# Phase two of a three-stage kernel: the sums of weight blocks on DVE instead of GpSimd

## The chip, the cores and the metric

One core of a Trainium2 chip runs the whole program. The metric is the device time of one execution in microseconds (us). Three executions of the kernel before took 1212.9, 1214.16 and 1216.59 us; the median is 1214.16 us.

The engines are called as the profile calls them: PE is TensorE (matmul), PEld its weight loads, DVE is VectorE, ACT is ScalarE, POOL is GpSimd, and SP issues the DMAs.

## The reference

A linear attention with decay is followed by two feed-forward layers. The last one is the second phase of the kernel, and the change lies there:

```python
def _moe2_ref(x, w_gate, w_val, w_out):      # x: 3072 x 512
    gate = 1.0 / (1.0 + np.exp(-(x @ w_gate)))   # 512 x 1536
    val = x @ w_val                              # 512 x 1536
    return (gate * val @ w_out).astype(np.float32)
```

Everything is float32 to the outside. The kernel splits each operand of a large product into a high and a low part and makes three matmuls of them (high by high, high by low, low by high).

## The kernel before

Phase one, to about 655 us of the trace, makes the attention and the first feed-forward layer, and writes its result to DRAM (`x2d`); it also converts the weights of the second layer to float32 and stores them (`w2d`). Phase two reads both back.

In phase two the products with `w_gate` and `w_val` are made by a Strassen-like scheme: seven block products instead of eight, on blocks of 256 columns of weights and on 512 tokens. For this it needs sums of blocks of the weights (S1 to S4) and sums of blocks of the activations (T1 to T4). The unit of work is a **chain**: one gate or value product for two feature blocks and 1024 tokens. There are 36 chains: 3 groups of 1024 tokens, 3 rounds in each, 4 chains in a round (gate, value, gate, value). A chain takes PE seven products of six matmuls, about 9.7 us. After the fourth chain of a round come the products with `w_out` (L651 to L653) for eight token tiles.

What a chain `n` does, in the order in which it is written out by hand (`manual_schedule`; each engine runs its instructions in that order):

- `load_chain(n)` (L493) lets SP issue two DMAs of the weights into one tile `raw8` of eight blocks. Two such tiles exist, one for even and one for odd chains.
- `sums(n)` (L503) makes the sums in place: S3 = A21 - A11 (L506, 256 columns), S1 and S2 in one instruction (L507, 512 columns), S4 = A12 - S2 (L510, 256 columns). Each needs the one before it.
- `split_chain(n, late)` (L512) splits the blocks: ACT rounds to the high part `oh` (L518), and the low part `ol` is the difference (L521). The early half (S1, S2, A11, A12; 1024 columns) has its difference on DVE, the late half (S3, A22, S4; 768 columns) on GpSimd.
- `begin(n)` makes the first product into a PSUM bank `pa`; `middle(n)` makes four more: into `pb`, into `pa` again (S2 by T2), into `pd`, into `pa` again (S3 by T3). Between the last two that use `pa`, ACT copies the bank out to a tile `u` (L588), so the S3 product has to wait for that copy. `finish(n)` makes the last two.
- The four results of a chain are `pb`, `c` (made of `pd` and a tile `u` by the DVE add of L538), `pa` and `pd`. For a gate chain ACT takes the sigmoid of each (L546). For a value chain each is multiplied by its gate on DVE (L555), rounded to `g2h` on ACT (L557), and the rest `g2l` is made on DVE (L559). `g2h` and `g2l` are the stationary operands of L651 to L653.
- The eight output tiles of a round rotate through three PSUM banks `po`; each is evicted by DVE or ACT (L655 to L668), so the fourth tile's products wait for the eviction of the first.
- `split_out2` (L637) splits a block of `w_out`: ACT makes `woh` (L640), GpSimd the low part `wol` (L641).

In iteration `n` of the loop at L798, `sums(n + 2)` is called behind `middle(n)` (L809), that is, right behind the add that makes `c` of chain `n`. For the fourth chain of a group's last round it is called between two evictions instead (L838). `sums(0)` is called in phase one (L780) and `sums(1)` at the border of the phases (L796). So 34 of the 36 calls lie in the loop: 9 in first chains, 9 in second, 8 in third, 6 in fourth chains, and 2 between evictions.

Of the kernel before, what the change touches and what calls it, by code (L numbers as in the profile page):

```python
# [13 lines left out]
ALU = mybir.AluOpType  # L14
# [10 lines left out]
def retention_moe_moe2(  # L25
# [12 lines left out]
    nc = tc.nc  # L38
# [374 lines left out]
    A21, S3, A22, S4, S1, S2, A11, A12 = range(8)  # L413
# [89 lines left out]
    def sums(n):  # L503

        t = wraw8[n]
        nc.gpsimd.tensor_tensor(out=t[:, S3], in0=t[:, A21], in1=t[:, A11], op=ALU.subtract)  # L506
        nc.gpsimd.tensor_tensor(  # L507
            out=t[:, S1:S2 + 1], in0=t[:, A21:S3 + 1], in1=t[:, A22:A22 + 1].to_broadcast([P, 2, 256]), op=ALU.add
        )
        nc.gpsimd.tensor_tensor(out=t[:, S4], in0=t[:, A12], in1=t[:, S2], op=ALU.subtract)  # L510

    def split_chain(n, late):  # L512

# [156 lines left out]
    with tc.manual_schedule():  # L670
# [56 lines left out]
        for i, (b, f) in enumerate(units):  # L727
# [50 lines left out]
            if b == len(blocks1) - 1:  # L778
                if f == 9:
                    sums(0)  # L780
                elif f in (11, 13):
                    split_chain(0, f == 13)()
# [11 lines left out]
        load_out(0)  # L794
        evict1(*units[-1])
        sums(1)  # L796
        xs = iter(())
        for n, (g, r, p, m) in enumerate(chains):  # L798
# [9 lines left out]
            if n + 2 < len(chains) and not (last and r == NR - 1):  # L808
                sums(n + 2)  # L809
# [117 lines left out]
```

## Time and profile before

| | us |
|---|---|
| median of three executions | 1214.16 |
| the profiled execution | 1213.36 |
| its span, first to last instruction | 1211.6 |
| PE busy | 1190.9 (98%) |
| DVE busy | 794.1 (66%) |
| ACT busy | 541.5 (45%) |
| POOL busy | 531.4 (44%) |

The span is 1.76 us shorter than the execution; that rest lies before the first and behind the last instruction. PE is busy nearly throughout, so an instruction on another engine matters only where PE comes to wait for it. Matmuls are pipelined: one is shown 0.39 us long, while the next one starts 0.23 us after it. PE's granted clock is full in all of phase two.

In a row of the timeline stand the start, the duration, the engine, the line, the operation, the tiles as output<-inputs, the shapes, and in brackets the idle time before it with what ended it. A row that ends in x2 is two instructions that followed each other.

### The profile page before, as it was taken

To read this page: it belongs to the slowest core of one execution; us is meant where nothing else is said; L and a number is where in the kernel's file an instruction comes from. 1 tells how busy PE (TensorE), PEld (TensorE's weight loads), DVE (VectorE), ACT (ScalarE), POOL (GpSimd) and SP (SyncE) were. 2 spreads that over 40 slices of the span, in tenths; PEclk is the share of its full clock that TensorE was granted. 3 is DMA by queue.
4 is the path that set the end of the run, shared out by engine and by line. 5 is a ranking of instruction groups with operands and counts; after the bars stand their busy time and mean duration, and the time that the engine had idled before them with its cause. 6 is when DMAs were issued, how large, how long until landed. Compare 5 with 4: busy or idle time off the path is not lost.

```text
span 1211.6 us, 16035 instructions
## 1 busy us (share of the span) xinstructions
PE 1190.9 (98%) x5916; PEld 953.2 (79%) x5916; DVE 794.1 (66%) x1049; ACT 541.5 (45%) x948; POOL 531.4 (44%) x398
## 2 busy tenths in 40 slices
PE   7999999999999999999999999999999999999998
PEld 6656878877788888788788888887888887888887
DVE  5989999686688677766663626367636458535454
ACT  5333444444444445444554526163626163626151
POOL 4556875222332332322454616166625256534340
PEclk8999999999999999999999999999999999999999
DMA  8554344534334334412102202043202142211111
GB/s 318 187 180 141 87 157 164 193 114 137 124 98 163 123 113 141 124 49 86 63 1 87 79 27 79 27 139 105 73 32 75 31 130 89 86 44 59 47 35 70
DMA packets 62431, 123.48 MB, mean 102 GB/s; under 512 B 6800, under 2 KB 16016, under 8 KB 62352
## 3 DMA queue, kind: packets, MB, share of 16 engines
q1 hardware_dynamic: 62352, 122.46, 31.0%
q8 instruction: 46, 0.75, 0.3%
q14 instruction: 33, 0.27, 0.1%
HBM read 98.31 MB, written 24.12 MB: 101 GB/s over the span
## 4 chain that ended last, share of the span: by engine, by line
PE 79%; DVE 10%; POOL 4%; issue 4%; DMA 2%; ACT 1%; SPq 0%; DVEq 0%; POOLq 0%; ACTq 0%
PE pa L529 14%; PE pd L529 7%; PE acc L377 6%; PE h L273 6%; PE h L272 6%; PE h L271 6%; PE acc L378 6%; PE acc L379 6%; PE po L651 4%; PE po L652 4%; PE po L653 4%; PE pb L529 3%; DVE cva L234 3%; PE h L142 2%; DVE cva L231 2%
## 5 line engine op out<-in xcount | busy, mean ns | idle before, releaser
L264 POOL TENSOR_TENSOR wl<-wraw,wh 128x512 fp32r<-128x512 f32 x112 | 163.5, 1466 | 300.8 <-ACT wh L263 300.4
L271 PE MATMUL h<-xh,wh 128*128 128x512 f32 x384 | 155.0, 404 | 0.7 <-ACT xh L187 0.7
L273 PE MATMUL h<-xh,wl 128*128 128x512 f32 x384 | 152.4, 397 | 2.2 <-POOL wl L264 1.9
L272 PE MATMUL h<-xl,wh 128*128 128x512 f32 x384 | 151.4, 394 | 0.2 <-DVE xl L188 0.2
L377 PE MATMUL acc<-gh,wh 128*128 128x512 f32 x352 | 142.2, 404 | 1.4 <-DVE half L396 1.4
L378 PE MATMUL acc<-gh,wl 128*128 128x512 f32 x352 | 137.9, 392 | 0.0
L379 PE MATMUL acc<-gl,wh 128*128 128x512 f32 x352 | 137.2, 390 | 0.0
L263 ACT CAST wh<-wraw 128x512 fp32r<-128x512 f32 x184 | 109.4, 616 | 35.5 <-PE acc L379 35.0
L521 POOL TENSOR_TENSOR ol<-raw,oh 128x768 fp32r<-128x768 f32 x36 | 68.0, 1889 | 127.1 <-ACT oh L518 127.1
L281 ACT ACTIVATE sg<-h 128x512 f32<-128x512 f32 x88 | 52.6, 598 | 146.6 <-PE h L273 146.4
L282 DVE TENSOR_TENSOR sg<-h,sg 128x512 f32<-128x512 f32 x88 | 60.6, 688 | 86.6 <-ACT sg L281 86.3
L651 PE MATMUL po<-woh,g2h 128*128 128x512 f32 x288 | 113.1, 393 | 2.8 <-DVE ost L538 2.8
L529 PE MATMUL pa<-xol,oh 128*128 128x512 f32 x288 | 114.0, 396 | 0.0
L529 PE MATMUL pa<-xoh,oh 128*128 128x512 f32 x288 | 113.3, 394 | 0.0
L529 PE MATMUL pa<-xoh,ol 128*128 128x512 f32 x288 | 112.8, 392 | 0.0
L652 PE MATMUL po<-wol,g2h 128*128 128x512 f32 x288 | 112.5, 390 | 0.0
L653 PE MATMUL po<-woh,g2l 128*128 128x512 f32 x288 | 112.3, 390 | 0.0
L287 ACT CAST gh<-sg 128x512 fp32r<-128x512 f32 x88 | 54.6, 621 | 98.1 <-DVE sg L282 98.1
L641 POOL TENSOR_TENSOR wol<-wor,woh 128x512 fp32r<-128x512 f32 x36 | 56.9, 1581 | 89.6 <-ACT woh L640 89.6
L273 PEld LDWEIGHTS h<-xh,wl 128*128 128x128 f32 x384 | 72.4, 189 | 21.7 <-POOL wl L264 5.2
L271 PEld LDWEIGHTS h<-xh,wh 128*128 128x128 f32 x384 | 72.7, 189 | 18.9 <-issue 1.0
L272 PEld LDWEIGHTS h<-xl,wh 128*128 128x128 f32 x384 | 72.5, 189 | 18.2 <-issue 1.9
(122 smaller groups left out, 2521.3 us busy)
## 6 DMA issues: line engine op xcount, KB each, us to landing
w<-in_w_dram SPq DMA_DIRECT2D x68, 512.0 KB, 3.7
in_t<-in_qkv_dram SPq DMA_DIRECT2D x96, 256.0 KB, 3.3
raw<-w2d SPq DMA_DIRECT2D x72, 256.0 KB, 3.1
w2d<-cva SPq DMA_DIRECT2D x36, 256.0 KB, 2.2
wor<-w2d SPq DMA_DIRECT2D x36, 256.0 KB, 2.7
out_dram<-ost SPq DMA_DIRECT2D x24, 256.0 KB, 2.0
xt<-x2d SPq DMA_DIRECT2D x18, 256.0 KB, 4.4
x2d<-ost SPq DMA_DIRECT2D x14, 256.0 KB, 2.9
```

Source lines behind the costliest of these rows:

```text
L263: nc.scalar.copy(wh, raw)
L264: lo_engine.tensor_tensor(out=wl, in0=raw, in1=wh, op=ALU.subtract)
L271: nc.tensor.matmul(bank[:, :n], wh[:, k, :], xh[:, k, :n], start=(k == 0), stop=False)
L272: nc.tensor.matmul(bank[:, :n], wh[:, k, :], xl[:, k, :n], start=False, stop=False)
L273: nc.tensor.matmul(bank[:, :n], wl[:, k, :], xh[:, k, :n], start=False, stop=(k == KC - 1))
L377: nc.tensor.matmul(a, wh[:, wc], gh[:, :n], start=st, stop=False)
L378: nc.tensor.matmul(a, wl[:, wc], gh[:, :n], start=False, stop=False)
L379: nc.tensor.matmul(a, wh[:, wc], gl[:, :n], start=False, stop=sp)
L529: nc.tensor.matmul(bank, w[:, kk], x[:, k, :], start=start and k == 0 and w is wh and x is xh, stop=stop and k == 1 and w is wl, skip_grou ...
L651: nc.tensor.matmul(bank, gh, wh, start=f == 0, stop=False)
L652: nc.tensor.matmul(bank, gh, wl, start=False, stop=False)
L653: nc.tensor.matmul(bank, gl, wh, start=False, stop=f == FR - 1)
```

## The change

All three instructions of `sums` are made on DVE (`nc.vector`) instead of GpSimd (`nc.gpsimd`). Operands, order and places of the calls stay.

```diff
     def sums(n):
 
         t = wraw8[n]
-        nc.gpsimd.tensor_tensor(out=t[:, S3], in0=t[:, A21], in1=t[:, A11], op=ALU.subtract)
-        nc.gpsimd.tensor_tensor(
+        nc.vector.tensor_tensor(out=t[:, S3], in0=t[:, A21], in1=t[:, A11], op=ALU.subtract)
+        nc.vector.tensor_tensor(
             out=t[:, S1:S2 + 1], in0=t[:, A21:S3 + 1], in1=t[:, A22:A22 + 1].to_broadcast([P, 2, 256]), op=ALU.add
         )
-        nc.gpsimd.tensor_tensor(out=t[:, S4], in0=t[:, A12], in1=t[:, S2], op=ALU.subtract)
+        nc.vector.tensor_tensor(out=t[:, S4], in0=t[:, A12], in1=t[:, S2], op=ALU.subtract)
```

## Rows read from the trace of the kernel before

**Rows 1.** Busy time by window in phase two; columns as in its first line.
```profile
core 0: us, PE busy (x) PEld busy (x) DVE busy (x) ACT busy (x) POOL busy (x), PEclk, DMA share, GB/s
640.00:800.00 160.00, 160.00 (x697) 130.62 (x696) 78.10 (x97) 70.33 (x116) 71.26 (x57) 1.00 0.20 61
800.00:1206.00 406.00, 403.19 (x1745) 326.68 (x1744) 223.29 (x282) 176.53 (x294) 189.43 (x144) 1.00 0.23 72
```

**Rows 2.** Waits of PE from 640 us on: total us, times, longest.
```profile
PE po L651 <- DVE ost L538: 2.8, 6, 0.9
```

**Rows 3.** Groups by line and shape, GpSimd: busy us, mean ns, idle before.
```profile
L507 POOL TENSOR_TENSOR raw<-raw 128x512 f32<-128x512 f32 x36 | 46.6, 1296 | 2.8
```

**Rows 4.** Three DVE lines: duration in ns, min/median/max, and shape.
```profile
L699 DVE TENSOR_TENSOR dv_sb<-dv_sb,dc_sb x4: 166/168/169, 9.2 to 9.8; 128x8 f32<-128x8 f32 x4
L254 DVE TENSOR_TENSOR cva<-cva,cvb x36: 676/684/690, 191.7 to 562.8; 128x512 f32<-128x512 f32 x36
L521 DVE TENSOR_TENSOR ol<-raw,oh x36: 1214/1215/1226, 629.6 to 1172.0; 128x1024 fp32r<-128x1024 f32 x36
```

**Rows 5.** Timeline of DVE and GpSimd where both want SBUF at once.
```profile
814.92 2.23 DVE L469 TENSOR_TENSOR xol<-xt,xoh 128x512 fp32r<-128x512 f32 x2
816.65 1.64 POOL L641 TENSOR_TENSOR wol<-wor,woh 128x512 fp32r<-128x512 f32 x1 [0.65 <-ACT woh L640]
817.07 1.77 DVE L555 TENSOR_TENSOR c<-c,sg 128x512 f32<-128x512 f32 x1
```

**Rows 6.** Timeline of PE where a bank came late.
```profile
830.41 0.39 PE L653 MATMUL po<-woh,g2l 128*128 128x512 f32 x1
831.18 0.50 PE L651 MATMUL po<-woh,g2h 128*128 128x512 f32 x1 [0.38 <-DVE ost L538]
831.98 0.40 PE L651 MATMUL po<-woh,g2h 128*128 128x512 f32 x1
```

**Rows 7.** Timeline of DVE in a fourth chain (group 1, round 1).
```profile
692.85 0.69 DVE L538 TENSOR_TENSOR c<-pd,u 128x512 f32<-128x512 f32 x1 [1.10 <-ACT u L598]
693.57 1.81 DVE L555 TENSOR_TENSOR c<-c,sg 128x512 f32<-128x512 f32 x1
696.34 0.70 DVE L555 TENSOR_TENSOR pa<-pa,sg 128x512 f32<-128x512 f32 x1 [0.96 <-PE pa L529]
697.70 0.69 DVE L559 TENSOR_TENSOR g2l<-pa,g2h 128x512 fp32r<-128x512 f32 x1 [0.65 <-ACT g2h L557]
700.99 0.68 DVE L661 COPY part<-po 128x512 f32<-128x512 f32 x1
```

**Rows 8.** GpSimd and ACT in that chain.
```profile
692.72 0.75 POOL L506 TENSOR_TENSOR raw<-raw 128x256 f32<-128x256 f32 x1 [0.81 <-DMA raw<-w2d]
693.45 0.62 ACT L640 CAST woh<-wor 128x512 fp32r<-128x512 f32 x1
```

**Rows 9.** PE's weight loads in that chain.
```profile
699.86 0.19 PEld L653 LDWEIGHTS po<-woh,g2l 128*128 128x128 f32 x1
702.80 0.19 PEld L651 LDWEIGHTS po<-woh,g2h 128*128 128x128 f32 x1
```

**Rows 10.** Timeline of DVE in a second chain (group 1, round 3).
```profile
788.59 0.70 DVE L538 TENSOR_TENSOR pd<-pd,u 128x512 f32<-128x512 f32 x1 [2.80 <-PE pd L529]
...
794.86 0.69 DVE L538 TENSOR_TENSOR c<-pd,u 128x512 f32<-128x512 f32 x1 [1.10 <-ACT u L598]
...
797.59 1.91 DVE L559 TENSOR_TENSOR g2l<-c,g2h 128x512 fp32r<-128x512 f32 x1
799.42 0.69 DVE L538 TENSOR_TENSOR pd<-pd,u 128x512 f32<-128x512 f32 x1
```

**Rows 11.** GpSimd, ACT and PE's weight loads in that chain and into the next.
```profile
797.10 1.85 POOL L521 TENSOR_TENSOR ol<-raw,oh 128x768 fp32r<-128x768 f32 x1
...
796.11 0.84 ACT L518 CAST oh<-raw 128x768 fp32r<-128x768 f32 x1
801.36 0.59 ACT L588 COPY u<-pa 128x512 f32<-128x512 f32 x1
...
802.08 0.19 PEld L529 LDWEIGHTS pa<-xoh,oh 128*128 128x128 f32 x1
```

## The prediction

> **What bounds the kernel now.** I read first how busy each engine is by window. In phase two PE is busy in all of the first 160 us and in all but 2.8 us of the next 406 us, at a granted clock of 1.00, the 2.4 GHz level [rows 1]. The view of waits says the same: PE waits 2.8 us in all, always for a bank that DVE has to evict [rows 2]. PE bounds this phase, and every other engine is hidden. So the change can gain next to nothing, and the question is whether it makes something late for PE that was in time. For that the timeline is read, chain by chain, with the times by which PE's weight loads needed each input.
>
> **What goes and what comes.** GpSimd loses 108 instructions: 36 of 1.30 us [rows 3] and 72 short ones of 0.75 us or a little more [rows 8]. None of them was waited for by PE. DVE gains them. An addition of 512 columns takes DVE 0.68 us. For 256 columns there is no row: the bounds are 0.17 us (8 columns) and 0.68 us (512 columns), and the line through the rows of 512 and 1024 columns gives 0.42 us [rows 4], which I take. A DVE instruction that needs its predecessor's result starts 0.03 us behind its end (the add of c and its multiplication [rows 7]), any other 0.08 us ahead of that end (817.07 against 814.92 + 2.23 [rows 5]). So the three sums hold DVE for about 1.5 us, 34 times in the loop. DVE's share there rises by some 50 us of 566, which is room enough on average; what counts is the place.
>
> **The wait that moves along.** S3 waits for the chain's weights, and with it now everything behind it on DVE: the multiplications and splits of the running chain, for which ACT and then PE wait. In the fourth chain, where the load came nearest, GpSimd started at 692.72 when the load had landed [rows 8]; DVE comes to S3 at 692.85 + 0.69 - 0.08 = 693.46 [rows 7]. That leaves 0.74 us, and the load is issued no later than now, since GpSimd, which frees its tile, has less to do. Cost: nothing; if that cover were gone, what it is late by would be added to the delays worked out below.
>
> **First and third chains (17 places).** Behind the sums DVE's next instruction waits 2.80 us for PE [rows 10], more than the 1.5 us of the sums. Cost: nothing. The four calls elsewhere (phase one, border, between evictions) also meet a DVE that waits for PE or ACT soon after; without that cover they would cost up to 4 x 1.5 = 6 us.
>
> **The rule between DVE and GpSimd.** Two rows decide the rest. GpSimd's subtraction came at 816.65 while DVE worked on the second of two subtractions (end 817.15), and took 1.64 us where it takes 1.30 us alone: it began at 816.99, 0.16 us before DVE's end, and DVE's next instruction, ready at 817.07, came only behind it and ended 0.55 us after GpSimd's end (818.84 against 818.29) [rows 5]. So two instructions with both inputs in SBUF exclude each other, and whoever asked first goes first, even between two back-to-back instructions of the other engine. The 0.16 us come out of the duration that I take for the free-running one, 1.30 us, as L507 takes [rows 3].
>
> The Trainium skill says in "SBUF — State Buffer", section "SBUF: two separate sides", that the engine that starts first holds the shared pair of ports for the whole instruction and the other fully blocks. The rows agree but for the end: GpSimd began 0.16 us before the recorded end of DVE's instruction [rows 5]. Taken to the letter the rule would add 0.16 us at each handover and make the sum below some 9 us instead of 6 us; I go by the rows.
>
> **Price of a late input.** The bank in the rows of PE came late: the weight load would have started with the matmul of 830.41 and started at 831.18, 0.77 us late. The matmul 0.23 us after 830.41 became 831.18 (0.54 late), and the next group of three began after 0.80 us instead of 0.68 us [rows 6]. The loss is 0.66 us, the lateness less 0.11 us. For the signal between two engines I add 0.06 us, an estimate, twice the 0.03 us inside DVE.
>
> **Fourth chains (6 places: rounds 1 and 2 of each group).** S3 runs 693.46 to 693.88, S1 and S2 693.91 to 694.60 [rows 4, 7]. Meanwhile ACT has `woh` ready at 694.07 [rows 8]; GpSimd, now free, asks at 694.13, gets the ports at 694.44 and holds them for 1.30 us, to 695.74. S4 waits for it and ends 0.42 - 0.14 us behind, at 696.02. GpSimd's next instruction, the late split (1.85 us [rows 11]), already waits in the same queue, goes in at 695.86 and ends at 697.71; the multiplication of c ends at 698.26, where it ended at 695.38 before. Behind it the multiplication of pa starts at 698.18 instead of 696.34 [rows 7]: its 0.96 us of slack is eaten and all that follows on DVE shifts by 1.84 us. So `g2l` of pa is there at 697.70 + 0.69 + 1.84 + 0.06 = 700.29; PE loads it at 699.86 [rows 9]: 0.43 us late, loss 0.32 us. The eviction of the first output tile ends at 700.99 + 0.68 + 1.84 = 703.51 [rows 7], with the signal 703.57; the fourth tile's first load stands at 702.80 + 0.32 = 703.12 [rows 9]: 0.45 us late, loss 0.34 us. Six times 0.66 us is **4.0 us**.
>
> **Second chains (9 places).** S3 runs 795.47 to 795.89, S1 and S2 to 796.61, S4 796.64 to 797.06; the multiplication of c is ready at 796.98 [rows 4, 10]. GpSimd's late split asks when ACT's `oh` is there, 796.11 + 0.84 + 0.06 = 797.01 [rows 11]: 0.03 us behind, so DVE goes first. The multiplication ends at 797.67, GpSimd runs 797.51 to 799.36, and DVE's `g2l` of c ends 0.55 us later, at 799.91, against 797.59 + 1.91 = 799.50 before [rows 10]. The chain pd add (799.42), its multiplication, ACT's cast and, behind the cast in ACT's queue, the copy `u` shifts by 0.41 us. The copy ends at 801.36 + 0.59 + 0.41 + 0.06 = 802.42; the load of the S3 product stands at 802.08 [rows 11]: 0.34 us late, loss 0.23 us. Nine times is **2.1 us**.
>
> **Sum.** 4.0 + 2.1 = 6.1 us. The profiled execution (1213.36 us, 1211.6 us of span and 1.76 us around it) would become 1219.5 us. It lay 0.8 us under the median; on the median of 1214.16 us I predict 1220.3 us, 0.5% slower. For 0.17 us per short sum the second chains cost nothing; for 0.68 us GpSimd gets ahead of DVE in them as well, which is the second rival.
>
> **Rivals.**
> 1. Not slower: in the fourth chain the multiplication of c follows S4 without letting the late split in. It then ends near 696.6, the multiplication of pa starts 0.2 us late, and both loads of PE keep their time. What is left is the second chains' 2.1 us or nothing: 1214.2 to 1216.3 us. For it speaks that PE hid all of this work so far, and that each lateness is under half a microsecond; against it the row in which GpSimd did slip in between [rows 5]. Chance 0.32.
> 2. GpSimd first in the second chains: 0.03 us is less than the error of three durations added up. If the late split asks before the multiplication of c is ready, it runs 797.01 to 798.86, the multiplication ends at 799.41, `g2l` of c waits for ACT's cast and runs to 800.79, the pd add starts at 800.71 instead of 799.42 [rows 10], and the copy is 1.22 us late: a loss of 1.11 us, nine times 10.0 us. With or without the fourth chains 1224.2 to 1228.2 us. Chance 0.22.
> 3. A gain: fewer collisions of GpSimd and DVE end the waits of PE in this phase. They are 2.8 us [rows 2] and stand around evictions that the change does not touch: 1211.4 us at best, from a phase that has nothing else to give. Chance 0.04.
>
> **How the numbers follow.** My case has 0.42; its own range, with lateness off by 0.1 us in every place, is 4 to 8 us. About 0.3%, 3.6 us, is what a measurement can tell from no change. Slower by more: my case but for 0.03, and rival 2, together 0.61. Within: rival 1 and the 0.03, together 0.35. Faster: 0.04. The range runs from rival 1's lower end to within the second's: 1214.0 to 1227.0 us; outside lie the gain, a little of rival 1 and the upper part of rival 2.
>
> **What the trace after would show.** Right: PE waits at L653 for DVE's `g2l` in six fourth chains, at L651 for the first eviction, and at L529 for ACT's `u` in nine chains, 0.2 to 0.4 us each; multiplications of c in fourth chains that end nearly 3 us later than now; DVE busy some 50 us more, GpSimd some 100 us less. Wrong: no new waits of PE (rival 1), or a multiplication of c in second chains that is shown over 2 us long behind GpSimd's L521 (rival 2). The prediction is also wrong if a short sum takes far from 0.42 us, or if DVE's S3 is seen waiting for its load.

## The result and the profile after

The changed kernel takes 1220.49 us in the median of four executions (1219.61 to 1222.21), the kernel before 1213.58 us beside it (1212.9 to 1216.59): ratio 1.0059, 95% interval 1.0047 to 1.0071, so 7 us slower. The profiled execution took 1220.41 us with a span of 1218.6 us.

What moved is seen first in the waits of PE's weight loads in phase two (from 640 us on; total us, times, longest). A weight load that comes late shows there even where the matmul behind it still hides a part.

```profile
PEld po L651 <- DVE ost L538: 6.3, 8, 1.5
PEld pa L529 <- ACT u L588: 3.6, 9, 0.4
PEld po L653 <- DVE g2l L559: 2.6, 6, 0.4
PEld po L651 <- ACT g2h L557: 1.5, 6, 0.5
PEld po L651 <- DVE part L538: 1.4, 3, 0.5
PEld po L651 <- DVE part L661: 1.4, 3, 0.5
```

The first line stood in the kernel before as well (6.0 us, 8 times; PE's own waits are [rows 2]). The others are new: nine waits for `u`, each at the S3 product of a third chain and made late by the second chain before it; six each for `g2l` and `g2h` in fourth chains, and six for the eviction of the first output tile there (three by a copy, three by an add).

The fourth chain that answers to [rows 7] and [rows 8], first DVE, then GpSimd (timeline: start, duration, engine, line, operation):

```profile
692.84 0.69 DVE L538 TENSOR_TENSOR c<-pd,u 128x512 f32<-128x512 f32 x1 [1.10 <-ACT u L598]
693.45 0.42 DVE L506 TENSOR_TENSOR raw<-raw 128x256 f32<-128x256 f32 x1
693.90 0.69 DVE L507 TENSOR_TENSOR raw<-raw 128x512 f32<-128x512 f32 x1
694.62 1.40 DVE L510 TENSOR_TENSOR raw<-raw 128x256 f32<-128x256 f32 x1
695.95 2.33 DVE L555 TENSOR_TENSOR c<-c,sg 128x512 f32<-128x512 f32 x1
698.20 0.69 DVE L555 TENSOR_TENSOR pa<-pa,sg 128x512 f32<-128x512 f32 x1
699.54 0.69 DVE L559 TENSOR_TENSOR g2l<-pa,g2h 128x512 fp32r<-128x512 f32 x1 [0.66 <-ACT g2h L557]
```

```profile
694.14 1.60 POOL L641 TENSOR_TENSOR wol<-wor,woh 128x512 fp32r<-128x512 f32 x1 [2.24 <-ACT woh L640]
695.71 2.02 POOL L521 TENSOR_TENSOR ol<-raw,oh 128x768 fp32r<-128x768 f32 x1
```

S4 (L510) is shown 1.40 us long, because it stood behind GpSimd's L641; the multiplication of c 2.33 us, because L521 had slipped in ahead of it. It ends at 698.28 instead of 695.38 [rows 7]. The weight loads of PE that this makes late, to be read against [rows 9]:

```profile
699.56 0.19 PEld L651 LDWEIGHTS po<-woh,g2h 128*128 128x128 f32 x1 [0.20 <-ACT g2h L557]
700.28 0.19 PEld L653 LDWEIGHTS po<-woh,g2l 128*128 128x128 f32 x1 [0.43 <-DVE g2l L559]
703.57 0.19 PEld L651 LDWEIGHTS po<-woh,g2h 128*128 128x128 f32 x1 [0.46 <-DVE part L661]
```

And the second chain that answers to [rows 10] and [rows 11], some 1.6 us later in the trace by what was lost ahead of it; DVE, then GpSimd, then the late weight load of the S3 product:

```profile
798.29 0.42 DVE L510 TENSOR_TENSOR raw<-raw 128x256 f32<-128x256 f32 x1
798.64 0.68 DVE L555 TENSOR_TENSOR c<-c,sg 128x512 f32<-128x512 f32 x1
...
800.01 1.57 DVE L559 TENSOR_TENSOR g2l<-c,g2h 128x512 fp32r<-128x512 f32 x1
```

```profile
798.68 2.35 POOL L521 TENSOR_TENSOR ol<-raw,oh 128x768 fp32r<-128x768 f32 x1 [3.11 <-PE pa L529]
```

```profile
804.09 0.19 PEld L529 LDWEIGHTS pa<-xoh,oh 128*128 128x128 f32 x1 [0.39 <-ACT u L588]
```

Here DVE's multiplication asked at 798.64, GpSimd at 798.68, and DVE went first; GpSimd's 2.35 us hold 0.5 us of waiting (alone it takes 1.85 us), and the split of c behind it is late all the same.

The loss itself is read from the starts of PE's matmuls in phase two: each step that is over 0.26 us counts with what it exceeds 0.23 us. Before, this gives 4.7 us, all at evictions in the two passages between groups. After, it gives 11.2 us: 2.15 us for the nine second chains (0.24 us each), 3.98 us at the six fourth chains (five of 0.62 us, one of 0.89 us) and 5.1 us in the passages. The span grew by 7.0 us: phase one is 0.3 us shorter, phase two 7.3 us longer, of which these waits are 6.5 us.

### The profile page after: what moved, and what is told of

Same layout as the page of the kernel before. It is cut to its first block, busy times and chain, and to the rows that moved or that the text cites. A ratio compares the mean times of both kernels' runs of the same rounds, so it can differ in the third digit from the quotient of the medians.

```text
span 1218.6 us, 15992 instructions
## 1 busy us (share of the span) xinstructions
PE 1195.7 (98%) x5916; PEld 948.0 (78%) x5916; DVE 850.9 (70%) x1157; ACT 542.0 (44%) x948; POOL 434.6 (36%) x290
## 4 chain that ended last, share of the span: by engine, by line
PE 82%; DVE 10%; issue 2%; POOL 2%; DMA 1%; ACT 1%; SPq 0%; DVEq 0%; ACTq 0%; POOLq 0%
PE pa L529 16%; PE pd L529 8%; PE acc L377 6%; PE h L273 6%; PE h L272 6%; PE h L271 6%; PE acc L378 6%; PE acc L379 6%; PE po L651 4%; PE po L653 4%; PE po L652 4%; PE pb L529 4%; DVE cva L234 2%; PE h L142 2%; DVE cva L231 2%
## 5 line engine op out<-in xcount | busy, mean ns | idle before, releaser
L521 POOL TENSOR_TENSOR ol<-raw,oh 128x768 fp32r<-128x768 f32 x36 | 73.5, 2043 | 253.6 <-ACT oh L518 211.7
L641 POOL TENSOR_TENSOR wol<-wor,woh 128x512 fp32r<-128x512 f32 x36 | 59.1, 1642 | 111.5 <-ACT woh L640 76.2
```

## Experiments

Each ran beside the kernel before on the same chip; ratios are against it, and one thousandth is 1.2 us. Line numbers in a kernel of an experiment can be some higher by its edit.

**Sums of fourth chains back on GpSimd.** `sums` takes the engine as an argument.

```diff
-                sums(n + 2)
+                sums(n + 2, nc.gpsimd if last else nc.vector)
```

> The six calls of sums in fourth chains are back on GpSimd, the other 28 stay on DVE. Theory (turns at the shared SBUF ports in fourth and second chains): the waits of PE's weight loads at L651 and L653 for g2h, g2l and the first eviction go, 4.0 us less than the changed kernel; the nine waits for u (L588) stay at 0.23 us loss each. About 3 us above the kernel before, ratio 1.002 to 1.003. Rival (what counts is DVE's longer queue, 0.2 us for each of the 34 calls wherever it stands): 28/34 of the 6.9 us stay, ratio 1.0047.

Measured: 1215.94 us, ratio 1.0022 (1.0013 to 1.0031). The waits of PE's weight loads are two:

```profile
PEld po L651 <- DVE ost L538: 6.2, 8, 1.5
PEld pa L529 <- ACT u L588: 3.5, 9, 0.4
```

All waits of fourth chains outside the passages are gone, the nine for `u` are as they were. Six of 34 calls carry 3.7 thousandths of the 5.9. A price of 0.2 us for each call, wherever it stands (1.0047), lies outside the interval.

**Sums of second chains back on GpSimd.**

```diff
-                sums(n + 2)
+                sums(n + 2, nc.gpsimd if m and not last else nc.vector)
```

> The nine calls of sums in second chains are back on GpSimd, the rest stays on DVE. Theory: the nine waits for u go, 2.1 us; the waits of fourth chains stay: about 4.8 us above the kernel before, ratio 1.004. Rival (0.2 us for each call): 25/34 of 6.9 us, 5.1 us, ratio 1.0042; time does not tell these two apart, the list of PE's waits does: under the rival the waits for u get fewer but do not vanish.

Measured: 1216.87 us, ratio 1.0032 (1.0022 to 1.0041). Now all nine waits for `u` are gone, and those of the fourth chains stand:

```profile
PEld po L651 <- DVE ost L538: 6.1, 8, 1.3
PEld po L653 <- DVE g2l L559: 2.6, 6, 0.4
...
PEld po L651 <- ACT g2h L557: 1.1, 6, 0.2
```

So the two losses are separate, and each goes with its own calls. The nine calls carry 2.7 thousandths; with the 3.7 of the fourth chains that is 6.4, and the whole is 5.9, which agrees within the intervals (some 0.9 to either side in each). The other 17 calls behind c's add, in first and third chains, made nothing late.

**The same DVE queue without GpSimd's subtraction.** In the six fourth chains the low part of one block of `w_out` is left out and filled with zeros, which reads nothing from SBUF.

```diff
-        nc.gpsimd.tensor_tensor(out=l, in0=raw, in1=h, op=ALU.subtract)
+        if zero:
+            nc.gpsimd.memset(l.bitcast(F32), 0.0)
+        else:
+            nc.gpsimd.tensor_tensor(out=l, in0=raw, in1=h, op=ALU.subtract)
...
-            split_out2()
+            split_out2(r < NR - 1)
             ob = {}
```

> As the changed kernel, all sums on DVE, but the low part of one w_out block in each of the six fourth chains (L641) is left out: GpSimd fills it with zeros, which reads nothing from SBUF. Theory: GpSimd no longer takes the ports between S1/S2 and S4, the multiplication of c ends about 0.9 us earlier, and the waits at L651 and L653 in fourth chains go though DVE's queue is as long as before: 4.0 us less than the changed kernel, ratio 1.002 to 1.003. Rival (length of DVE's queue): nothing changes, ratio 1.0059.

Measured: 1216.79 us, ratio 1.0026 (1.0017 to 1.0036). In the six fourth chains no weight load waits any more, though DVE does the same as in the changed kernel. The nine waits for `u` stay, and so do waits in the passages; in the first of these one load now waits 1.18 us for `g2h`, behind a multiplication of c that took 2.33 us there. DVE and GpSimd in the chain shown above:

```profile
694.46 0.69 DVE L538 TENSOR_TENSOR c<-pd,u 128x512 f32<-128x512 f32 x1 [1.10 <-ACT u L598]
...
695.52 2.22 DVE L507 TENSOR_TENSOR raw<-raw 128x512 f32<-128x512 f32 x1
...
698.11 0.69 DVE L555 TENSOR_TENSOR c<-c,sg 128x512 f32<-128x512 f32 x1
```

```profile
695.24 1.95 POOL L521 TENSOR_TENSOR ol<-raw,oh 128x768 fp32r<-128x768 f32 x1 [1.25 <-ACT oh L518]
```

One collision is left, at another place than I expected: the late split asks during S3 and goes ahead of S1/S2. But one is not enough: c's multiplication ends 4.3 us behind the start of c's add, where it took 5.4 us in the changed kernel and 2.5 us before [rows 7], and no weight load comes late for it. The loss of the fourth chains is two of GpSimd's instructions in a row that get between DVE's, and not the length of DVE's queue.

**GpSimd asks earlier.** In second chains ACT's cast for the late split is written out ahead of `begin`; DVE's instructions stay as they are.

```diff
-                begin(n + 1)
-                rest = split_chain(n + 1, True)
+                if m:
+                    rest = split_chain(n + 1, True)
+                    begin(n + 1)
+                else:
+                    begin(n + 1)
+                    rest = split_chain(n + 1, True)
                 finish(n, False)
```

> As the changed kernel, but in second chains ACT's cast for the late split is written out ahead of begin, so that GpSimd's late split asks for the ports about 1.4 us earlier, during the sums; DVE's instructions and their order are the same. Theory (who asks first goes first): the split gets between S3 and S1/S2, S4 and the multiplication of c follow 0.6 us later, u is 1.0 us late at nine places, loss 0.9 us each instead of 0.23: 6 us above the changed kernel, ratio 1.011. Rival (the order at the ports does not matter, only the work on DVE): no change against the changed kernel, ratio 1.0059.

Measured: 1226.15 us, ratio 1.0107 (1.0093 to 1.0121). DVE and GpSimd in a second chain, and the wait for `u` in all of them:

```profile
798.35 2.21 DVE L507 TENSOR_TENSOR raw<-raw 128x512 f32<-128x512 f32 x1
800.60 0.42 DVE L510 TENSOR_TENSOR raw<-raw 128x256 f32<-128x256 f32 x1
800.94 0.68 DVE L555 TENSOR_TENSOR c<-c,sg 128x512 f32<-128x512 f32 x1
```

```profile
798.07 1.94 POOL L521 TENSOR_TENSOR ol<-raw,oh 128x768 fp32r<-128x768 f32 x1 [1.71 <-ACT oh L518]
```

```profile
PEld pa L529 <- ACT u L588: 9.2, 9, 1.0
```

GpSimd's split asked while S3 ran, and the whole of it came before S1/S2 (2.21 us instead of 0.69). Each second chain loses 0.87 us by the steps of PE's matmuls, against 0.24 us. I expected c's multiplication 0.6 us later, and it came 1.5 us later; but the split of c behind it no longer met GpSimd (0.69 us instead of 1.57 us), so `u` was late by 0.63 us more than in the changed kernel. The same work in the same order on DVE costs 5.8 us more because the other engine asked 1.4 us earlier. The edit also puts ACT's copy `m` behind that cast, but this is not what made `u` late: ACT's copy `u` stands behind a cast that waited 0.58 us for DVE's multiplication of pd.

**One short sum twice.** In second chains S4 is made a second time.

```diff
-        nc.vector.tensor_tensor(out=t[:, S4], in0=t[:, A12], in1=t[:, S2], op=ALU.subtract)
+        for _ in range(1 + again):
+            nc.vector.tensor_tensor(out=t[:, S4], in0=t[:, A12], in1=t[:, S2], op=ALU.subtract)
...
-                sums(n + 2)
+                sums(n + 2, again=m == 1 and not last)
```

> As the changed kernel, but in the nine second chains S4 is made twice by DVE (the same sum into the same place): 0.42 us of DVE work more at each place. Theory (who asks first goes first): the late split, which now asks 0.04 us behind the multiplication of c, comes ahead of the second S4, and the whole 1.85 us of it stand before the multiplication; u is about 1.5 us later than in the kernel before, loss 1.3 to 1.4 us for each place instead of 0.23: 10 us above the changed kernel, ratio 1.014. Rival (only the length of DVE's queue counts): 0.45 us for each place, 4 us above the changed kernel, ratio 1.009.

Measured: 1229.88 us, ratio 1.0136 (1.0122 to 1.0150). The pair of S4 and what follows it on DVE, and GpSimd's late split (L522 here):

```profile
673.54 2.51 DVE L511 TENSOR_TENSOR raw<-raw 128x256 f32<-128x256 f32 x2
675.97 0.68 DVE L556 TENSOR_TENSOR c<-c,sg 128x512 f32<-128x512 f32 x1
```

```profile
673.92 1.84 POOL L522 TENSOR_TENSOR ol<-raw,oh 128x768 fp32r<-128x768 f32 x1 [3.05 <-PE pa L530]
```

The pair takes 2.51 us instead of some 0.9: the split came between the two. By the rows the second S4, which follows the first by 0.03 us, can ask at 673.54 + 0.42 + 0.03 = 673.99, and GpSimd asked at 673.92. Each second chain loses 1.43 us, 1.19 us more than with one S4, for 0.42 us of work. So the order of asking sets the price; in the changed kernel, at 0.24 us, DVE was ahead by 0.04 us.

**Sums ahead of c's add.** All 32 calls behind c's add are moved ahead of it, into the time in which DVE waits for `u`.

```diff
+        if n + 2 < len(chains) and not (chains[n][2:] == (PAIRS - 1, 1) and chains[n][1] == NR - 1):
+            sums(n + 2)
         add(c22, d, u3)
...
-            if n + 2 < len(chains) and not (last and r == NR - 1):
-                sums(n + 2)
```

> All sums on DVE, but called ahead of c's add instead of behind it, in all 32 places of the loop that stand there: DVE waits 0.8 to 1.1 us for ACT's u before that add in second, third and fourth chains. Theory: the sums fill that wait, c's add is at most 0.6 us later, the multiplication of c keeps ahead of the late split and of pa's product, and neither u nor g2l comes late: the 6 us of the change go, ratio 1.000 to 1.001. Rival (DVE's 50 us of work cost wherever they stand): 1.006. If the weights have not landed by then, S3 waits and c's add with it; then PE would be seen waiting for c at the S4 product.

Measured: 1218.73 us, ratio 1.0045 (1.0033 to 1.0058): missed. The waits of second and fourth chains are gone, but a new one stands in eight third chains and three first ones. The list, then DVE and GpSimd in a third chain:

```profile
PEld pd L529 <- DVE c L538: 7.6, 11, 0.8
```

```profile
802.37 1.21 DVE L521 TENSOR_TENSOR ol<-raw,oh 128x1024 fp32r<-128x1024 f32 x1
803.50 1.52 DVE L506 TENSOR_TENSOR raw<-raw 128x256 f32<-128x256 f32 x1
```

```profile
802.37 2.36 POOL L643 TENSOR_TENSOR wol<-wor,woh 128x512 fp32r<-128x512 f32 x1 [3.59 <-ACT woh L642]
```

GpSimd's subtraction asked at the same time as DVE's L521, waited for it, and then stood ahead of S3, which took 1.52 us instead of 0.42 us. So c's add came too late for the S4 product, which adds to the same bank. S3 takes 1.51 or 1.52 us in all eight third chains. It is the rule of the other runs again, at a place where I had not looked for it.

The three first chains, one at the start of each group, have another cause: no instruction of GpSimd runs beside S3, which waited for its weights, which the expectation had named as a risk:

```profile
848.64 0.43 DVE L506 TENSOR_TENSOR raw<-raw 128x256 f32<-128x256 f32 x1 [2.60 <-DMA raw<-w2d]
```

By the steps of PE's matmuls the third chains lose some 4.8 us, the first ones 0.9 us. In both kinds of chain the place of the change, behind c's add, is the better one.

**Sums placed by chain.** All on DVE: first and third chains as in the change, second chains ahead of c's add, fourth chains behind the second eviction.

```diff
+        if chains[n][2:] == (0, 1):
+            sums(n + 2)
         add(c22, d, u3)
...
-            if n + 2 < len(chains) and not (last and r == NR - 1):
+            if n + 2 < len(chains) and m == 0:
                 sums(n + 2)
...
-                if tt == 5 and n + 2 < len(chains) and r == NR - 1:
+                if tt == (5 if r == NR - 1 else 1) and n + 2 < len(chains):
                     sums(n + 2)
```

> All sums on DVE; in first and third chains where the change has them, in second chains ahead of c's add, in fourth chains of rounds 1 and 2 behind the second eviction, where DVE waits for PE. Theory: no wait of PE that the kernel before did not have, ratio 1.000 (within 0.001). Rival: 1.006, as the changed kernel.

Measured: 1213.68 us against 1213.65 us, ratio 1.0000 (0.9991 to 1.0008). The only wait left is the one of the kernel before:

```profile
PEld po L653 <- DVE ost L538: 6.2, 8, 1.4
```

The same 108 instructions on the same engine cost 7 us or nothing (within some 1 us), by their place alone.

**The eighth load earlier.** What is left of PE's waits in phase two stands in the passages between groups. In the kernel `placed`, SP, ACT and DVE there:

```profile
825.74 6.64 SPq L670 DMA_DIRECT2D out_dram<-ost  x3
832.48 0.37 SPq L449 DMA_DIRECT2D xt<-x2d  x1
```

```profile
836.12 1.66 ACT L468 CAST xoh<-xt 128x512 fp32r<-128x512 f32 x3 [9.36 <-DMA xt<-x2d]
```

```profile
836.77 1.29 DVE L469 TENSOR_TENSOR xol<-xt,xoh 128x512 fp32r<-128x512 f32 x2 [3.07 <-ACT xoh L468]
837.98 0.68 DVE L538 TENSOR_TENSOR ost<-po,part 128x512 f32<-128x512 f32 x1
```

One load of activations stands on SP's queue behind stores that wait for evictions; the casts and then DVE's splits wait for it, and the next eviction stands behind the splits. The edit issues it ahead of the stores:

```diff
-                load(1, *((B21,) if g else (B11, B12, B22, B21)))
+                if not g:
+                    load(1, B11, B12, B22, B21)
                 yield
...
             split(B11, nc.vector)
+            if g and not k:
+                load(1, B21)
             yield
```

> As placed, and in the two passages from one group of tokens to the next the eighth load of activations is issued about 15 us earlier, ahead of the output stores on SP's queue, which it stood behind. In the kernel before ACT waits 9.3 us for it there, DVE's split behind it holds up an eviction, and PE loses 1.1 us at each passage. Expected: PE's longest wait for an eviction (0.9 us) goes in both passages, 2 us less than placed, ratio 0.998. Rival (the eviction waits for the other splits on DVE anyway): as placed, 1.000.

Measured: 1207.89 us, ratio 0.9954 (0.9941 to 0.9968): 5.6 us less than the kernel before by the ratio, where 2 us were expected. No wait of PE is left in phase two; not the longest one alone went, but all. SP after the edit:

```profile
811.05 0.43 SPq L449 DMA_DIRECT2D xt<-x2d  x1
821.19 15.69 SPq L673 DMA_DIRECT2D out_dram<-ost  x8
```

The load is issued 21 us earlier than in `placed`, and DVE's wait of 3.07 us for the cast is gone; that answers for the longest wait, as expected. The splits still stand between the evictions, but the first two of them take 1.28 us (at 821.09) instead of 2.37 us (at 825.63). Why the shorter waits, which come ahead of the late load, went as well was not tested further. Whether this gain needs the sums on DVE was asked by one more run, the kernel before with this edit alone.

> The kernel before (all sums on GpSimd), with the early issue of the eighth load of activations as its only edit. It tells how much of the 0.46% of the run placed_load is the load's alone. If the load alone: all waits of PE for evictions go (4.7 us in the profile), ratio 0.995 to 0.996. If GpSimd has to be rid of the sums in the passages as well: some of these waits stay, since GpSimd's own sums and differences of activations then still stand in one queue and take turns with DVE's splits; ratio 0.997 to 0.999.

Measured: 1208.07 us against 1212.94 us, ratio 0.9958 (0.9944 to 0.9971). No wait of PE is left in phase two there either. The load alone gives as much as both edits together, within the intervals; the sums may stay on GpSimd. Both versions beat the kernel before and the changed one.

## Why the prediction was right

- **PE bounds phase two, and the change cannot gain.** Right. GpSimd was relieved of 97 us (531.4 to 434.6 us), DVE got 57 us (794.1 to 850.9 us), and nothing became faster; 17 calls in first and third chains made no wait at all.
- **The short sum: 0.42 us.** Taken from the line through the rows of 512 and 1024 columns, drawn on to 256; measured 0.416 us (L506) and 0.425 us (L510) in the median:

```profile
L506 DVE TENSOR_TENSOR raw<-raw x36: 408/416/421, 618.2 to 1171.6; 128x256 f32<-128x256 f32 x36
L510 DVE TENSOR_TENSOR raw<-raw x36: 424/425/1403, 620.5 to 1172.8; 128x256 f32<-128x256 f32 x36
```

- **S3's wait for its load** was costed at nothing, and DVE was never seen idle for it: GpSimd's late split is earlier by what left its queue, and with it the load (issued at 687.13 instead of 688.17 in the fourth chain shown). The run with the sums ahead of c's add shows that this term can come due: there S3 waited for its weights at three places, 7.8 us in all.
- **Fourth chains, 4.0 us:** measured 3.98 us, in part by luck: five places lose 0.62 us, one 0.89 us, and the forecast had 0.66 us for each. c's multiplication was forecast to end at 698.26 and ended at 698.28. One input was missed: the cast `g2h` of pa is late as well, by 0.20 us, and takes part of the loss that I put on `g2l`; at the one place with 0.89 us it was 0.48 us late. Both waits of the forecast were there, 0.43 and 0.46 us long.
- **Second chains, 2.1 us:** measured 2.15 us. Two small errors cancel: the load was 0.39 us late instead of 0.34 us, and lost 0.15 us less than that instead of 0.11 us less. DVE asked 0.04 us ahead of GpSimd, forecast 0.03 us. This step was right by a margin that no sum of rows can carry for sure; the run with S4 twice shows the other outcome, 1.4 us at each place, where rival 2's 1.11 us and the second S4's 0.42 us make 1.5 us.
- **The rule at the ports** carried both terms, and the experiments show it: the loss goes when GpSimd's instruction reads nothing, and grows by 5.8 us when GpSimd asks earlier. The Trainium skill, in "SBUF — State Buffer", section "SBUF: two separate sides", lets the holder keep the ports for the whole instruction. To the letter this gave the forecast some 9 us (with 0.16 us more only where DVE hands over to GpSimd); measured were 6.1 us. In the row of L641 after, 1.60 us for 1.30 us alone from 694.14 on, GpSimd began at 694.44 if its work took 1.30 us here too, 0.15 us before DVE's recorded end (693.90 + 0.69). Whether DVE still held the ports then, or GpSimd needed them from its start, no run shows.
- **Rival 1** fell with the row of L521 after: GpSimd did slip in between S4 and the multiplication. **Rival 2** did not happen in the changed kernel. **Rival 3** was right in that the change takes nothing from these waits, but its ceiling of 2.8 us was read too low: by the steps of PE's matmuls the same waits cost 4.7 us, and the kernel before without them (`before_load`) is 4.9 us faster.
- **Not in the sum:** 0.35 us more at evictions in the passages, and about 0.8 us in steps of PE that are each too small to show as a wait. Where these come from stays open. Against the interval of the ratio, 5.7 to 8.6 us, they cannot be told from nothing. That the median came out within 0.2 us of the forecast 1220.3 us is chance: the kernel before was 0.6 us faster in the median of four than in the three runs that the forecast started from, and about as much of the loss was not in the sum.

## What to carry to other kernels

Work that moves to an engine with room on average is paid for by its place: write out what is queued behind it, by when the next engine needs that, and which other engine's instruction asks for the same ports in between. Look at the order of asking, not only at busy shares; here equal calls cost nothing, 0.24 us or some 0.6 us each, and in second chains the lead behind the price was 0.04 us. And where the bounding engine is 98% busy, look for the few waits that it still has: issuing one load ahead of the stores that it stood behind gave some 5 us, while the moved work gave nothing at the best of the places tried.

## What the runs showed of the hardware

DVE and GpSimd, where both read two inputs from SBUF, take turns in the order in which they ask (as the starts in the profile show it), and a waiting engine gets in between two back-to-back instructions of the other: S4 was stretched from 0.42 to 1.40 us and the multiplication behind it from 0.68 to 2.33 us by two of GpSimd's instructions. A lead of 0.04 us was enough in all nine second chains. With one input in PSUM nothing of the kind is seen: DVE's add of pd and `u` ran beside GpSimd's L521 at 18 places of the changed kernel and took 0.70 us at most. A weight load that comes late costs PE some 0.15 us less than its wait: 0.39 us of waiting, 0.24 us lost (second chains of the changed kernel); 1.02 us, 0.87 us lost (GpSimd asks earlier); 1.59 us, 1.43 us lost (S4 twice). The forecast had 0.11 us from one place.
